# Attention and two mixtures on one core: q, k and v in longer runs, the weights' clamp as two operations, the norm's refinement in two instructions

## The chip, the cores and the metric

The kernel runs on one core of one Trainium2 chip. The metric is the device time of one execution in microseconds (us). Each kernel was run three times; the median is quoted. Beside the timed runs one execution was profiled; its trace is what is read here.

## What is computed

Three steps follow one another. Shapes: q, k and v are 4 x 8 x 576 x 64 (batch, head, token, dimension), the token matrix is 2304 x 512.

```python
def _attn_ref(q, k, v, g_norm):
    kv = np.einsum('bhsd,bhse->bhde', k, v)
    out = np.einsum('bhsd,bhde->bhse', q, kv)
    rms = np.sqrt(np.mean(out * out, axis=-1, keepdims=True) + 1e-06)
    return (out / rms * g_norm).astype(np.float32)

def _moe_ref(x, w1, w2, w3, w_out):          # 512 -> 768 -> 512
    h = np.maximum(np.maximum(x @ w1, x @ w2), x @ w3)
    return (h @ w_out).astype(np.float32)

def _moe2_ref(x, domain_probs, w1, w2):      # 4 experts, 512 -> 1024 -> 512
    p = domain_probs / (domain_probs.sum(-1, keepdims=True) + 1e-09)
    out = np.zeros((N, D), dtype=np.float32)
    for e in range(E):
        h = np.maximum(x @ w1[e], 0.0)
        out += p[:, e:e + 1] * (h @ w2[e])
    return out.astype(np.float32)
```

The weights of the middle step arrive as 64-bit floats, all other inputs as 32-bit floats.

## The kernel before

The kernel has one fixed order of work. A list of short step names (`steps`, near the end of the program) sets the order in which all engines get their instructions up to about 150 us; behind it come the long loops of matrix products, which the change doesn't touch.

**Loads.** After each step `pump()` issues whatever loads the list `order` has next, as long as a buffer is free: `kbc` is the load of k and v for batch b and the c-th four heads (`load_kv`), `qn` the load of the n-th group of queries (`load_q`), `w` the next weight of the middle step. All go through SP's queue, apart from v's first half, which goes through ACT's. There are three pairs of k/v buffers and six q buffers. The program's waits also hold every load until the one issued eight loads before it has landed.

**How q, k and v lie in the chip's memory.** 576 tokens are 4.5 times 128. For k and v, partition p holds the four tokens 4p to 4p+3 of each head, one run of 1 KB, and the last 64 tokens go to the first 64 partitions in a second, small load of 256 B runs. For q a group is 256 tokens of one batch, partition p holding two tokens, a run of 512 B; the last 64 tokens of all four batches form group 2, the tail, loaded by four DMAs to 32 partitions each.

**Attention steps.** `Kbc` (`att_kv`) forms k-transposed times v for a pair of heads: ten matmuls, five chunks of tokens times two heads. Behind the last pair of a batch its result is copied into `kvb`. `Tn` (`att_T`) transposes the queries of group n on PE and copies them out; for the tail POOL first reorders them into `qr`. `On` (`att_O`) multiplies them with `kvb`, squares on ACT and sums on DVE, and forms `a`, the mean square plus epsilon. `Nn` (`att_N`) takes the inverse root: ACT's square root `s0`, DVE's reciprocal, one refinement `s0 + a/s0` (two instructions), another reciprocal, and the scaling. `Xn` (`att_X`) transposes the result back for the next step, and `Sj` splits it into a high and a low part.

**Weights.** A weight goes through `c` (`conv0`: ACT takes the absolute value of the upper words, POOL clamps them), `d` (`conv1`: DVE builds the 32-bit float with three instructions) and `s` (`conv2`: split into two parts on ACT, POOL or DVE). There are 24 weights, c0 to c23; c0 runs at 11 us, c1 and c2 near 46 us, the others between 64 and 152 us, beside the products of the middle step (steps A, H, P).

The output rows: `tiles` holds, for each 128-row tile, the rows of `out` it is written to; the token order within a batch follows that of q. The probabilities are loaded in the same order by `load_probs`.

Of the kernel before, what the change touches and what calls it, by code (L numbers as in the profile page):

```python
# [21 lines left out]
def tile_attn_moe_moe2(  # L22
# [109 lines left out]
    def load_q(pool, gi):
        b, s0, _ = groups[gi]
        t = pool.tile([P, H, 2, D], F32, tag="q", name=f"q{gi}", bufs=6)
        if s0 is None:
            n = P // B
            for bb in range(B):
                nc.sync.dma_start(
                    out=t[bb * n : (bb + 1) * n], in_=q[bb, :, SB:S, :].rearrange("h (p r) d -> p h r d", r=2)
                )  # L140
        else:
            nc.sync.dma_start(
                out=t, in_=q[b, :, s0 : s0 + 256, :].rearrange("h (p r) d -> p h r d", r=2)
            )
        q_sb[gi] = t

    HALF = P // 2
    KS = P * KC  # L150

    def load_first(pool):

        ends = []
        for src, nm, eng in ((k, "k", nc.sync), (v, "v", nc.scalar)):
            t = pool.tile([P, 4, KC + 1, D], F32, tag="kv", name=f"{nm}0_0", bufs=6)
            rows = src[0, 0:4]
            parts = [
                (t[:, 2 * i : 2 * i + 2, 0:KC, :], rows[2 * i : 2 * i + 2, 0:KS, :].rearrange("h (p c) d -> p h c d", c=KC))
                for i in range(2)  # L160
            ]
            eng.dma_start(out=parts[0][0], in_=parts[0][1])
            eng.dma_start(out=t[0:HALF, :, KC, :], in_=rows[:, KS:S, :].rearrange("h p d -> p h d"))
            ends.append(parts[1])
            kv_sb[nm, 0, 0] = t
# [3 lines left out]
    def load_kv(pool, b, c):
        if (b, c) == (0, 0):  # L170
            return load_first(pool)
        for src, nm in ((k, "k"), (v, "v")):
            t = pool.tile([P, 4, KC + 1, D], F32, tag="kv", name=f"{nm}{b}_{c}", bufs=6)
            rows = src[b, 4 * c : 4 * c + 4]
# [97 lines left out]
    def att_kv(kvb, b, c, eng=""):  # L272
        if c == 0:
            kv_ps[b] = banks[7]
        ps = kv_ps[b]
        kt, vt = kv_sb["k", b, c // 2], kv_sb["v", b, c // 2]
        for i in range(KC + 1):
            for h in range(2):
                o = ps[h * D : (h + 1) * D, c * D : (c + 1) * D]
                n = P if i < KC else HALF  # L280
                hh = c % 2 * 2 + h
                nc.tensor.matmul(o, kt[0:n, hh, i, :], vt[0:n, hh, i, :], start=(i == 0), stop=(i == KC))
        if c == NPAIR - 1:
            dst = kvb[b % 2][:, 0 : H * P].rearrange("p (c h n) -> p c h n", h=2, n=P)
            for h in range(2):
                src = ps[h * D : (h + 1) * D, 0 : NPAIR * D].rearrange("p (c e) -> p c e", e=D)
                e = eng[2 * h :] or "aa"
                copy(e[0], dst[0:D, :, h, 0:D], src)
                copy(e[1], dst[D:P, :, h, D:P], src)

    qT = {}
    TAIL = 2
    xtok = {}

    def att_T(pool, gi, eng="aa"):


        pair = groups[gi][1] is None
        t = pool.tile([P, 4, P, 2] if pair else [P, 2, 4, P], F32, tag="qp" if pair else "qT", name=f"qT{gi}", bufs=1 if pair else 2)
        qs = q_sb.pop(gi)  # L300
        if pair:
            qr = pool.tile([P, 2, H, D], F32, tag="qr", name="qr", bufs=1)
            nc.gpsimd.tensor_copy(out=qr, in_=qs.rearrange("p h r d -> p r h d"))
        for i in range(2):
            ps = bank("a").rearrange("p (c n) -> p c n", n=P)
            for c in range(4):
                src = qr[:, i, 2 * c : 2 * c + 2, :] if pair else qs[:, 4 * i + c, :, :]
                nc.tensor.transpose(ps[:, c, :], src, ident)
            copy(eng[i], t[:, :, :, i] if pair else t[:, i], ps)
        qT[gi] = t  # L310

    def att_O(pool, kvb, gi):
        b, s0, _ = groups[gi]
        qt = qT[TAIL] if s0 is None else qT.pop(gi)
        ps = [bank("acc") for i in range(1 if s0 is None else 2)]
        xt = pool.tile([P, 2, H, D], F32, tag="xt", name=f"xt{gi}", bufs=3)
        if s0 is None:
            nbank = 1
            for c in range(NPAIR):
# [19 lines left out]
        def small(nm):  # L339
            return smp.tile([P, nbank, 8], F32, tag=nm, name=f"{nm}{gi}")  # L340

        ss, a = small("ss"), small("a")
        for i in range(nbank):
            sq = xt[:, i]
            nc.scalar.activation(out=sq, in_=o[i], func=AF.Square)
            nc.vector.reduce_sum(out=ss[:, i, :], in_=sq, axis=AX.X)
        nc.vector.tensor_scalar(out=a, in0=ss, scalar1=1.0 / D, scalar2=EPS, op0=ALU.mult, op1=ALU.add)
        xtok[gi] = (xt, ss, a, o, dst, small)

    def att_N(gi):  # L350
        xt, ss, a, o, dst, small = xtok[gi]
# [42 lines left out]
    nm = [0]  # L394
# [80 lines left out]
    first = [1]  # L475
# [424 lines left out]

    def norm_probs():
# [374 lines left out]
```

## Time and profile before

| what | value |
|---|---|
| median of 3 runs | 1102.78 us (1101.92 to 1104.07) |
| the profiled execution | 1102.58 us |
| its span in the trace | 1100.8 us |
| PE busy | 1070.6 us (97%) |
| DVE busy | 768.7 us (70%) |
| ACT busy | 593.9 us (54%) |
| POOL busy | 238.8 us (22%) |
| DMA queue of SP | 89,248 packets, 169.34 MB |

PE is the matrix engine, PEld its weight loads, DVE the vector engine, ACT the scalar engine, POOL GpSimd; SPq is SP's queue, which issues DMAs. The shares are means over the whole span. The first 62 us are attention; until 150 us the middle step runs beside the conversion of its weights; everything behind that is matrix products. Rows of the trace name lines of the program, as L282, and in brackets the time for which the engine stood idle before a row and what ended the wait.

### The profile page before, as it was taken

To read this page: it belongs to the slowest core of one execution; us is meant where nothing else is said; L and a number is where in the kernel's file an instruction comes from. 1 tells how busy PE (TensorE), PEld (TensorE's weight loads), DVE (VectorE), ACT (ScalarE), POOL (GpSimd) and SP (SyncE) were. 2 spreads that over 40 slices of the span, in tenths; PEclk is the share of its full clock that TensorE was granted. 3 is DMA by queue.
4 is the path that set the end of the run, shared out by engine and by line. 5 is a ranking of instruction groups with operands and counts; after the bars stand their busy time and mean duration, and the time that the engine had idled before them with its cause. 6 is when DMAs were issued, how large, how long until landed. Compare 5 with 4: busy or idle time off the path is not lost.

```text
span 1100.8 us, 19219 instructions
## 1 busy us (share of the span) xinstructions
PE 1070.6 (97%) x7318; PEld 1051.7 (96%) x7318; DVE 768.7 (70%) x1434; ACT 593.9 (54%) x1257; POOL 238.8 (22%) x269
## 2 busy tenths in 40 slices
PE   7889999999999989999999999999999999999997
PEld 6779999999999879999999999999999999999997
DVE  3889985667656879776676666667667666666556
ACT  3544224335343666665665566666566566556652
POOL 1336633330101101111202212212212220221121
PEclk8999999999999999999999999999999999999999
DMA  9945555431610877388569579759949957956875
GB/s 259 295 148 162 181 182 178 132 119 53 210 58 20 328 270 266 142 311 240 90 221 272 119 169 285 182 100 290 250 77 277 277 86 227 271 116 166 235 222 115
DMA packets 109820, 209.17 MB, mean 190 GB/s; under 512 B 13856, under 2 KB 67104, under 8 KB 109728
## 3 DMA queue, kind: packets, MB, share of 16 engines
q1 hardware_dynamic: 89248, 169.34, 46.4%
q0 software_dynamic: 19472, 37.76, 19.2%
q8 instruction: 57, 0.93, 0.3%
q10 hardware_dynamic: 1008, 0.85, 0.3%
q14 instruction: 35, 0.29, 0.1%
HBM read 137.93 MB, written 69.99 MB: 189 GB/s over the span
## 4 chain that ended last, share of the span: by engine, by line
PE 63%; DVE 0%; issue 0%; DVEq 0%
PE bank L878 32%; PE bank L617 30%; DVE wr L579 0%; DVE xr L500 0%; DVE fa L861 0%; DVE hr L653 0%; DVE hr L651 0%; DVEq L1271 0%
## 5 line engine op out<-in xcount | busy, mean ns | idle before, releaser
L878 PE MATMUL bank<-wr 128*128 128x256 f32 x1701 | 263.5, 283 | 0.4 <-DVE wr L579 0.4
L878 PEld LDWEIGHTS bank<-wr 128*128 128x128 f32 x1701 | 239.9, 190 | 0.6 <-DVE wr L579 0.6
L617 PE MATMUL bank<-rb,wl 128*128 128x384 f32 x1032 | 211.6, 340 | 4.2 <-DVE rb L500 2.3
L671 ACT ACTIVATE fa<-bank 128x384 f32<-128x384 f32 x192 | 94.7, 493 | 171.4 <-PE bank L617 169.5
L617 PEld LDWEIGHTS bank<-rb,wl 128*128 128x128 f32 x1032 | 176.0, 189 | 7.4 <-DVE rb L500 3.5
L617 PE MATMUL bank<-xr,wl 128*128 128x384 f32 x864 | 175.8, 337 | 1.7 <-DVE xr L500 1.1
L617 PEld LDWEIGHTS bank<-xr,wl 128*128 128x128 f32 x864 | 144.9, 188 | 3.6 <-DVE xr L500 2.5
L653 DVE TENSOR_TENSOR wr<-fa,wr 128x384 fp32r<-128x384 f32 x131 | 72.3, 552 | 50.8 <-ACT wr L646 50.7
L878 PE MATMUL bank<-wr,hr 128*128 128x256 f32 x558 | 91.0, 281 | 0.0
L836 POOL DMA_DIRECT2D out_dram<-w2s x48 | 48.1, 1027 | 193.0 <-DVE ob L861 145.0
L836 POOL DMA_DIRECT2D out_dram<-ob x48 | 47.7, 1033 | 166.8 <-DVE w2s L861 90.6
L878 PEld LDWEIGHTS bank<-wr,hr 128*128 128x128 f32 x558 | 80.5, 188 | 0.0
L646 ACT ACTIVATE wr<-fa 128x384 fp32r<-128x384 f32 x152 | 78.2, 529 | 2.0 <-DVE fa L661 0.5
L878 PE MATMUL bank<-wr,xr 128*128 128x256 f32 x405 | 67.9, 281 | 0.0
L760 DVE TENSOR_TENSOR fa<-bank,fa 128x384 f32<-128x384 f32 x54 | 29.9, 554 | 51.8 <-ACT fa L757 36.5
L836 POOL DMA_DIRECT2D out_dram<-fa x37 | 34.2, 1054 | 123.9 <-DVE fa L861 68.9
L694 DVE TENSOR_TENSOR fa<-bank,fa 128x384 f32<-128x384 f32 x48 | 26.7, 557 | 49.2 <-PE bank L617 49.2
L683 DVE TENSOR_TENSOR fa<-bank,fa 128x384 f32<-128x384 f32 x48 | 26.7, 557 | 48.0 <-ACT fa L671 47.2
L859 ACT ACTIVATE ob<-bank,p_all 128x256 f32<-128x256 f32 x102 | 48.3, 474 | 21.7 <-PE bank L878 20.0
L859 ACT ACTIVATE w2s<-bank,p_all 128x256 f32<-128x256 f32 x104 | 49.3, 474 | 18.8 <-PE bank L878 18.7
L617 PE MATMUL bank<-op,wl 128*128 128x384 f32 x288 | 58.7, 339 | 0.6 <-ACT fa L671 0.6
L878 PEld LDWEIGHTS bank<-wr,xr 128*128 128x128 f32 x405 | 59.0, 188 | 0.0
(207 smaller groups left out, 2041.9 us busy)
## 6 DMA issues: line engine op xcount, KB each, us to landing
rb<-op_d SPq DMA_DIRECT2D x42, 768.0 KB, 5.1
xr<-op_d SPq DMA_DIRECT2D x42, 768.0 KB, 7.0
out_dram<-w2s POOLq DMA_DIRECT2D x47, 256.0 KB, 5.9
out_dram<-ob POOLq DMA_DIRECT2D x46, 256.0 KB, 5.2
op<-op_d SPq DMA_DIRECT2D x14, 768.0 KB, 7.9
stage_a<-in_moe_w_dram SPq DMA_DIRECT2D x18, 512.0 KB, 4.0
w1s<-in_moe_w_dram SPq DMA_DIRECT2D x30, 256.0 KB, 3.6
out_dram<-fa POOLq DMA_DIRECT2D x30, 256.0 KB, 5.9
```

The costliest lines, as they stand in the source:

```text
L617: nc.tensor.matmul(out, w[wi][:, c * P : (c + 1) * P], y[yi][:, c, :], start=(i == 0 and k in begin), stop=(i == 5), skip_group_check=k no ...
L646: nc.scalar.activation(out=ops[key][0], in_=src, func=AF.Relu if relu else AF.Copy)
L653: nc.vector.tensor_tensor(out=lo, in0=src, in1=f32(hi), op=ALU.subtract)
L671: nc.scalar.activation(out=out, in_=in_, func=func)
L683: nc.vector.tensor_tensor(out=t22, in0=x, in1=t22, op=ALU.add)
L694: nc.vector.tensor_tensor(out=t12, in0=x, in1=t12, op=ALU.add)
L760: nc.vector.tensor_tensor(out=mx[done] if i == 0 else t, in0=x, in1=t, op=ALU.add)
L836: nc.gpsimd.dma_start(out=rows, in_=src, accum_op=ALU.add)
L859: nc.scalar.activation(out=o, in_=piece(ps, i), func=AF.Copy, scale=pe)
L878: nc.tensor.matmul(piece(ps, i), h[hi][:, i * P : (i + 1) * P], w[wi], start=fresh, stop=last, skip_group_check=True,)
```

## The change

Four things are edited, all in the part up to 150 us.

- **k and v**: partition p of 96 holds the six tokens 6p to 6p+5 of each head, one run of 1.5 KB. The small second load is gone; `att_kv` has twelve matmuls (six chunks times two heads), each over 96 partitions.
- **q**: one tile holds a whole batch's first 512 tokens, partition p four of them, a run of 1 KB, loaded in two DMAs of four heads each; it serves two groups. There are three such tiles. The tail is loaded in eight DMAs with 256 B runs, already in the order that the transposes want, so POOL's copy `qr` goes. The list `order` is shortened to match; `out`'s rows and the probabilities follow the new order of tokens (rows 8 KB apart instead of 4 KB, still 2 KB each).
- **The clamp** on POOL: `min` becomes `min` and then `max` with 0.0, which changes no value, since these are absolute values.
- **The norm**: `a` is no longer formed; the refinement is two instructions of the form (x op constant) op y, the first one from the sum `ss` itself.

The core of the diff:

```diff
-    KC = S // P
+    KC = 6
+    KP = S // KC
...
     def load_q(pool, b):
+        if b == B:
+            t = pool.tile([P, 2, H, D], F32, tag="qe", name="q_ends", bufs=1)
             n = P // B
             for bb in range(B):
+                for r in range(2):
+                    nc.sync.dma_start(
+                        out=t[bb * n : (bb + 1) * n, r],
+                        in_=q[bb, :, SB:S, :].rearrange("h (p r) d -> r p h d", r=2)[r],
+                    )
+            q_sb[TAIL] = t
+            return
+        t = pool.tile([P, H, 4, D], F32, tag="q", name=f"q{b}", bufs=3)
+        for i in range(2):
+            hs = slice(i * H // 2, (i + 1) * H // 2)
+            nc.sync.dma_start(out=t[:, hs], in_=q[b, hs, 0:SB, :].rearrange("h (p r) d -> p h r d", r=4))
...
+    def load_kv(pool, b, c):
...
+            t = pool.tile([P, 4, KC, D], F32, tag="kv", name=f"{nm}{b}_{c}", bufs=6)
+            rows = src[b, 4 * c : 4 * c + 4].rearrange("h (p c) d -> p h c d", c=KC)
...
+                nc.sync.dma_start(out=t[0:KP], in_=rows)
-            nc.sync.dma_start(out=t[:, :, 0:KC, :], in_=rows[:, 0:KS, :].rearrange("h (p c) d -> p h c d", c=KC))
-            nc.sync.dma_start(out=t[0:HALF, :, KC, :], in_=rows[:, KS:S, :].rearrange("h p d -> p h d"))
...
-        nc.gpsimd.tensor_scalar(out=t, in0=t, scalar1=EXP_TOP, scalar2=None, op0=ALU.min)
+        nc.gpsimd.tensor_scalar(out=t, in0=t, scalar1=EXP_TOP, scalar2=0.0, op0=ALU.min, op1=ALU.max)
...
-                nc.tensor.matmul(o, kt[0:n, hh, i, :], vt[0:n, hh, i, :], start=(i == 0), stop=(i == KC))
+                nc.tensor.matmul(o, kt[0:KP, hh, i, :], vt[0:KP, hh, i, :], start=(i == 0), stop=(i == KC - 1))
...
-            nc.gpsimd.tensor_copy(out=qr, in_=qs.rearrange("p h r d -> p r h d"))
...
-        nc.vector.tensor_scalar(out=a, in0=ss, scalar1=1.0 / D, scalar2=EPS, op0=ALU.mult, op1=ALU.add)
...
-        nc.vector.tensor_tensor(out=rr, in0=a, in1=rr, op=ALU.mult)
-        nc.vector.tensor_tensor(out=rr, in0=rr, in1=s0, op=ALU.add)
+        nc.vector.scalar_tensor_tensor(out=rr, in0=ss, scalar=EPS * D, in1=rr, op0=ALU.add, op1=ALU.mult)
+        nc.vector.scalar_tensor_tensor(out=rr, in0=rr, scalar=1.0 / D, in1=s0, op0=ALU.mult, op1=ALU.add)
...
-            "w k00 k01 q1 q0 k10 q3 q2 k11 q4 q5 k20 w q6 k21 w k30 k31 q8 w q9"
+            "w k00 k01 q0 k10 q4 k11 q1 k20 w q2 k21 w k30 k31 w q3"
...
-        free = {"q": 6, "k": 3}
+        free = {"q": 4, "k": 3}
```

The edit of the load list moves loads on SP's queue. Before, from the first queries to the loads that step K12 needs (k_0 and k_1 are names of buffers, a number behind a DMA's shape says how often it is issued):

```order
L142 DMA q_193<-in_q_dram 128x8x128
L142 DMA q_195<-in_q_dram 128x8x128
L175 DMA k_0_197<-in_k_dram 128x4x256
L176 DMA k_0_197<-in_k_dram 64x4x64
L175 DMA v_0_200<-in_v_dram 128x4x256
L176 DMA v_0_200<-in_v_dram 64x4x64
L142 DMA q_203<-in_q_dram 128x8x128
L138 DMA q_205<-in_q_dram 32x8x128 x4
L175 DMA k_1_233<-in_k_dram 128x4x256
L176 DMA k_1_233<-in_k_dram 64x4x64
L175 DMA v_1_236<-in_v_dram 128x4x256
L176 DMA v_1_236<-in_v_dram 64x4x64
```

The same stretch of SP's queue with the change, up to the second batch's queries:

```order
L151 DMA q_189<-in_q_dram 128x4x256 x2
L165 DMA k_0_192<-in_k_dram 96x4x384
L165 DMA v_0_194<-in_v_dram 96x4x384
L142 DMA q_ends<-in_q_dram 32x8x64 x8
L165 DMA k_1_232<-in_k_dram 96x4x384
L165 DMA v_1_234<-in_v_dram 96x4x384
L151 DMA q_236<-in_q_dram 128x4x256 x2
```

Step T3's queries were q_203, 512 KB ahead of the tail and of K12's k and v; now they are half of q_236, 1 MB behind both.

On PE the steps X1, T2, T3, K12 and K13, before:

```order
L375 MATMUL bank_71<-ident,xt_294 128x128 x4
L375 MATMUL bank_72<-ident,xt_294 128x128 x4
L308 MATMUL bank_70<-ident,qr 128x128 x4
L308 MATMUL bank_71<-ident,qr 128x128 x4
L308 MATMUL bank_72<-ident,q_203 128x128 x4
L308 MATMUL bank_70<-ident,q_203 128x128 x4
L282 MATMUL bank_73<-v_1_236,k_1_233 64x64 x20
```

and with the change:

```order
L360 MATMUL bank_71<-ident,xt_293 128x128 x4
L360 MATMUL bank_72<-ident,xt_293 128x128 x4
L294 MATMUL bank_70<-ident,q_ends 128x128 x4
L294 MATMUL bank_71<-ident,q_ends 128x128 x4
L294 MATMUL bank_72<-ident,q_236 128x128 x4
L294 MATMUL bank_70<-ident,q_236 128x128 x4
L272 MATMUL bank_73<-v_1_234,k_1_232 64x64 x24
```

PE's order of steps is the same; K12 and K13 grow from 20 matmuls to 24 and stay behind T3, whose queries now come last.

On DVE the sums of groups 2 and 4 and the start of N2, before (`a` is L347):

```order
L346 TENSOR_REDUCE ss_493<-xt_484 128x8
L347 TENSOR_SCALAR a_494<-ss_493 128x8
L346 TENSOR_REDUCE ss_528<-xt_519 128x8 x2
L347 TENSOR_SCALAR a_529<-ss_528 128x16
L356 RECIPROCAL rr_539<-s_538 128x8
L357 TENSOR_TENSOR rr_539<-a_494,rr_539 128x8
L358 TENSOR_TENSOR rr_539<-rr_539,s_538 128x8
```

and with the change:

```order
L332 TENSOR_REDUCE ss_488<-xt_479 128x8
L332 TENSOR_REDUCE ss_523<-xt_514 128x8 x2
L341 RECIPROCAL rr_532<-s_531 128x8
L342 SCALAR_TENSOR_TENSOR rr_532<-ss_488,rr_532 128x8
L343 SCALAR_TENSOR_TENSOR rr_532<-rr_532,s_531 128x8
```

One small instruction of each of the ten groups leaves DVE's queue; nothing else on it moves.

## Rows read from the trace of the kernel before

**Rows 1.** Busy time by stretch: length, then PE, PEld, DVE, ACT, POOL, clock, DMA, GB/s

```profile
10.00:20.00 10.00, 7.40 (x62) 6.56 (x63) 2.50 (x4) 2.55 (x6) 1.73 (x2) 0.66 1.13 288
38.00:62.00 24.00, 20.78 (x264) 18.18 (x264) 22.66 (x50) 12.39 (x27) 7.63 (x7) 1.00 1.13 307
62.00:150.00 88.00, 83.59 (x498) 80.74 (x499) 82.79 (x131) 34.25 (x62) 51.72 (x41) 0.98 0.51 159
```

**Rows 2.** PE's waits from 0 to 62 us: total, times, longest

```profile
PE bank L282 <- DMA v<-in_v_dram: 5.9, 5, 2.9
PE bank L308 <- POOL qr L303: 1.8, 1, 1.8
```

**Rows 3.** DMA view of single microseconds, from 5, 8, 13 and 22 us

```profile
DMA packets 622, 0.25 MB, mean 252 GB/s; under 512 B 491, under 2 KB 622, under 8 KB 622
DMA packets 343, 0.35 MB, mean 350 GB/s; under 512 B 1, under 2 KB 343, under 8 KB 343
DMA packets 607, 0.30 MB, mean 304 GB/s; under 512 B 14, under 2 KB 607, under 8 KB 607
DMA packets 403, 0.20 MB, mean 196 GB/s; under 512 B 20, under 2 KB 403, under 8 KB 403
```

**Rows 4.** DMA view: us to landing of the issues at 8.58 and 24.43

```profile
v<-in_v_dram SPq DMA_DIRECT2D x1, 64.0 KB, 4.3
v<-in_v_dram SPq DMA_DIRECT2D x1, 64.0 KB, 6.5
```

**Rows 5.** Timeline of SP's queue: start, us, line

```profile
8.58 0.61 SPq L176 DMA_DIRECT2D v<-in_v_dram  x1
...
24.43 0.61 SPq L176 DMA_DIRECT2D v<-in_v_dram  x1
```

**Rows 6.** Timeline of PE: steps K02 and K03, T3, K12 and K13, X6

```profile
12.58 2.98 PE L282 MATMUL bank<-v,k 128*64 128x64 f32 x40 [2.94 <-DMA v<-in_v_dram]
...
29.07 1.12 PE L308 MATMUL bank<-ident,q 128*128 128x128 f32 x8
30.58 1.82 PE L282 MATMUL bank<-v,k 128*64 128x64 f32 x40 [0.39 <-DMA v<-in_v_dram]
...
63.21 1.10 PE L375 MATMUL bank<-ident,xt 128*128 128x128 f32 x6 [2.09 <-ACT qT L69]
```

**Rows 7.** Timeline of POOL and DVE around the norm's `a`

```profile
37.06 1.26 POOL L210 TENSOR_TENSOR wl<-cv_a,wl 128x512 fp32r<-128x512 f32 x1
37.43 0.92 DVE L347 TENSOR_SCALAR a<-ss 128x16 f32<-128x16 f32 x1
38.27 1.74 DVE L389 TENSOR_TENSOR xr<-fa,xr 128x1536 fp32r<-128x1536 f32 x1
...
54.94 0.83 DVE L347 TENSOR_SCALAR a<-ss 128x16 f32<-128x16 f32 x1
56.98 0.17 DVE L347 TENSOR_SCALAR a<-ss 128x16 f32<-128x16 f32 x1
61.70 0.43 DVE L71 COPY kvb<-bank 64x256 f32<-64x256 f32 x1
```

**Rows 8.** Groups by line and shape, 0 to 160 us: busy, mean ns, idle before

```profile
L225 POOL TENSOR_SCALAR cv_a<-cv_a 128x512 f32<-128x512 f32 x18 | 28.7, 1592 | 32.4 <-ACT cv_a L224 31.7 <-DVE fa L405 0.7
L71 POOL CAST wr<-cv_o 128x512 fp32r<-128x512 f32 x3 | 1.8, 607 | 0.0
L210 POOL TENSOR_TENSOR wl<-cv_a,wl 128x512 fp32r<-128x512 f32 x6 | 8.0, 1338 | 0.8 <-ACT wl L69 0.4
L233 DVE SCALAR_TENSOR_TENSOR cv_a<-stage_a,cv_a 128x512 int32<-128x512 int32 x18 | 14.7, 817 | 0.6
L236 DVE SCALAR_TENSOR_TENSOR cv_o<-stage_o,cv_o 128x512 int32<-128x512 int32 x6 | 4.1, 691 | 0.2
```

**Rows 9.** PE's waits from 62 to 150 us: total, times, longest

```profile
PE bank L375 <- ACT qT L69: 2.1, 1, 2.1
PE bank L260 <- DVE fa L405: 1.5, 2, 1.3
PE bank L375 <- DVE xt L366: 0.9, 1, 0.9
PE bank L424 <- DVE xt L366: 0.8, 1, 0.8
```

More of the change, by code (lines that the diff above doesn't have):

```diff
@@ L59, in tile_attn_moe_moe2 @@
     NPAIR = H // 2
-    KC = S // P
+    KC = 6
+    KP = S // KC
     EPS = 1e-6
+    HALF = P // 2
     WARM = 16
@@ L118, in tile_attn_moe_moe2 @@
     groups = []
-    SB = S // 256 * 256
+    SB = S // 512 * 512
+    TAIL = 2
+    by_r = [out[b * S : b * S + SB, :].rearrange("(p r) d -> r p d", r=4) for b in range(B)]
     for b0 in range(0, B, 2):
@@ L125, in tile_attn_moe_moe2, with load_q @@
             else:
-                rows = out[b * S + s0 : b * S + s0 + 256, :].rearrange("(p r) d -> r p d", r=2)
-                tiles += [[rows[0]], [rows[1]]]
+                r0 = s0 // P
+                tiles += [[by_r[b][r0]], [by_r[b][r0 + 1]]]
     q_sb = {}
     kv_sb = {}
[L132 to L135, printed above, removed]
+    def load_q(pool, b):
+        if b == B:
+            t = pool.tile([P, 2, H, D], F32, tag="qe", name="q_ends", bufs=1)
@@ L136, in load_q @@
             n = P // B
             for bb in range(B):
[L138 to L152, printed above, removed]
-        ends = []
[L155 to L165, printed above, removed]
+                for r in range(2):
[3 more added lines that the diff above has]
+                    )
@@ new lines, in load_q @@
+            q_sb[TAIL] = t
[4 more added lines that the diff above has]
+            nc.sync.dma_start(out=t[:, hs], in_=q[b, hs, 0:SB, :].rearrange("h (p r) d -> p h r d", r=4))
+        for n, gi in enumerate(gi for gi, g in enumerate(groups) if g[0] == b and g[1] is not None):
+            q_sb[gi] = t[:, :, 2 * n : 2 * n + 2, :]
+    def load_kv(pool, b, c):
+        first = (b, c) == (0, 0)
+        ends = []
+        for src, nm in ((k, "k"), (v, "v")):
+            t = pool.tile([P, 4, KC, D], F32, tag="kv", name=f"{nm}{b}_{c}", bufs=6)
+            rows = src[b, 4 * c : 4 * c + 4].rearrange("h (p c) d -> p h c d", c=KC)
+            if first:
+                (nc.sync if nm == "k" else nc.scalar).dma_start(out=t[0:KP, 0:2], in_=rows[:, 0:2])
+                ends.append((t[0:KP, 2:4], rows[:, 2:4]))
+            else:
+                nc.sync.dma_start(out=t[0:KP], in_=rows)
+            kv_sb[nm, b, c] = t
@@ L166, in load_first @@
         for o, i in ends:
             nc.sync.dma_start(out=o, in_=i)
[L169 to L174, printed above, removed]
-            nc.sync.dma_start(out=t[:, :, 0:KC, :], in_=rows[:, 0:KS, :].rearrange("h (p c) d -> p h c d", c=KC))
-            nc.sync.dma_start(out=t[0:HALF, :, KC, :], in_=rows[:, KS:S, :].rearrange("h p d -> p h d"))
-            kv_sb[nm, b, c] = t
@@ L276, in att_kv @@
         kt, vt = kv_sb["k", b, c // 2], kv_sb["v", b, c // 2]
-        for i in range(KC + 1):
+        for i in range(KC):
             for h in range(2):
                 o = ps[h * D : (h + 1) * D, c * D : (c + 1) * D]
-                n = P if i < KC else HALF
                 hh = c % 2 * 2 + h
-                nc.tensor.matmul(o, kt[0:n, hh, i, :], vt[0:n, hh, i, :], start=(i == 0), stop=(i == KC))
+                nc.tensor.matmul(o, kt[0:KP, hh, i, :], vt[0:KP, hh, i, :], start=(i == 0), stop=(i == KC - 1))
         if c == NPAIR - 1:
@@ L291, in tile_attn_moe_moe2 @@
     qT = {}
-    TAIL = 2
     xtok = {}
@@ L300, in att_T @@
         qs = q_sb.pop(gi)
-        if pair:
-            qr = pool.tile([P, 2, H, D], F32, tag="qr", name="qr", bufs=1)
-            nc.gpsimd.tensor_copy(out=qr, in_=qs.rearrange("p h r d -> p r h d"))
         for i in range(2):
@@ L306, in att_T @@
             for c in range(4):
-                src = qr[:, i, 2 * c : 2 * c + 2, :] if pair else qs[:, 4 * i + c, :, :]
+                src = qs[:, i, 2 * c : 2 * c + 2, :] if pair else qs[:, 4 * i + c, :, :]
                 nc.tensor.transpose(ps[:, c, :], src, ident)
@@ L340, in small @@
             return smp.tile([P, nbank, 8], F32, tag=nm, name=f"{nm}{gi}")
-        ss, a = small("ss"), small("a")
+        ss = small("ss")
         for i in range(nbank):
@@ L346, in att_O @@
             nc.vector.reduce_sum(out=ss[:, i, :], in_=sq, axis=AX.X)
-        nc.vector.tensor_scalar(out=a, in0=ss, scalar1=1.0 / D, scalar2=EPS, op0=ALU.mult, op1=ALU.add)
-        xtok[gi] = (xt, ss, a, o, dst, small)
+        xtok[gi] = (xt, ss, o, dst, small)
     def att_N(gi):
-        xt, ss, a, o, dst, small = xtok[gi]
+        xt, ss, o, dst, small = xtok[gi]
         nbank = len(o)
@@ L895, in load_probs @@
             else:
-                r0 = b * S + s0
+                r0 = s0 // P
                 nc.sync.dma_start(
-                    out=p_all[:, t : t + 2, :], in_=probs[r0 : r0 + 256, :].rearrange("(p r) e -> p r e", r=2)
+                    out=p_all[:, t : t + 2, :],
+                    in_=probs[b * S : b * S + SB, :].rearrange("(p r) e -> p r e", r=4)[:, r0 : r0 + 2, :],
                 )
@@ L926, in tile_attn_moe_moe2 @@
         order = (
-            "w k00 k01 q1 q0 k10 q3 q2 k11 q4 q5 k20 w q6 k21 w k30 k31 q8 w q9"
+            "w k00 k01 q0 k10 q4 k11 q1 k20 w q2 k21 w k30 k31 w q3"
         ).split()
-        free = {"q": 6, "k": 3}
+        free = {"q": 4, "k": 3}
+        got = set()
         def pump():
@@ L997, in tile_attn_moe_moe2 @@
                 att_T(xq, *at, *en)
-                free["q"] += 1
+                mate = {0: 1, 1: 0, 3: 4, 4: 3, 5: 6, 6: 5, 8: 9, 9: 8}.get(at[0])
+                got.add(at[0])
+                free["q"] += mate in got
             elif kind == "K":
```

## The prediction

> **What bounds the kernel now.** I read the stretches first. Beyond 150 us the change touches no instruction of PE, which is 97% busy over the span, so the question is how much earlier or later that part starts. Between 62 and 150 us PE is busy for 83.6 of 88 us and DVE for 82.8 [rows 1]: both are nearly full, and a shift at 62 us is passed on to the end, with no slack to swallow it. From 38 to 62 us DVE is busy for 22.7 of 24 us [rows 1] and runs without a wait from 38.27 to the copy at 61.70 [rows 7]; PE then waits 2.09 us for what that copy frees [rows 6]. So DVE is the bound there, and PE (20.8 of 24) isn't. Before 38 us neither is full: PE waits 5.9 us for v, most of it once, at 12.58, and 1.8 us for POOL's copy of the tail [rows 2, 6]. There the chain runs through PE's order: T2, T3, K12 and K13, then X0 and the split whose last instruction is DVE's at 38.27. What this chain gains or loses stays to the end.
>
> **Prices of a load.** In a microsecond in which the 16 DMA engines are busy, 16,000 ns divided by the packets is what one packet takes of an engine: 1 KB 16,000/343 = 46.6 ns, 512 B 16,000/607 = 26.4 ns, and 256 B (16,000 - 131 x 46.6)/491 = 20.2 ns [rows 3]. By the step from 512 B to 1 KB, 1.5 KB would take 66.8 ns, an estimate. One load of k or v was 512 packets of 1 KB and 256 of 256 B, 29.0 us of engine time or 1.81 us on sixteen engines. It becomes 384 packets of 1.5 KB: 1.60 us, if 96 partitions cost nothing. At 22 us, where the tail's DMAs run, each over 32 partitions, the same 512 B packets moved at 196 GB/s instead of 304 [rows 3]: a quarter of the partitions, 0.645 of the rate. Two thirds of the way back to 128 partitions is 0.88, which makes 1.82 us; in proportion to the partitions it would be 2.13 us. I take 1.82, nearest to the only row on fewer partitions: k and v gain nothing. Ends 1.60 and 2.13.
>
> [...]
>
> **T3's queries.** Before, the last data on this chain was K12's v: ahead of it a weight (512 packets, 1.49 us), eight loads of k and v (14.5), three groups of q (1024 x 26.4/16 = 1.69 each, 5.1) and the tail (524 KB at 196 GB/s, 2.7), 23.8 us together. It was issued at 24.43 and landed 6.5 later, at 30.9 [rows 4, 5], 7.1 behind the sum. Now T3, ahead of K12 on PE, needs the whole second batch: a weight 1.49, eight loads 14.6, two batches of q (1024 x 46.6/16 = 2.98 each, 6.0) and the tail 2.7, 24.8 us. With the same lag it lands at 31.9. But at 12.9 (8.58 + 4.3) [rows 4, 5] the lag was only 12.9 - 1.49 - 4 x 1.81 = 4.2; the other 2.9 came between, while half of the eight loads in flight were small ones. Now they are large, the tail's eight aside; I give half of it back: 30.4. The second half of T3 ran at about 29.6 [rows 6], so T3 is 0.8 late. K12 and K13 take 1.82 us for 40 rows, so 48 take 2.18, another 0.4 [rows 6]. **X0 and DVE's run: 1.2 us later.** Ends: lag 4.2 at 1.60 us a load gives 27.2, so 2.0 us earlier; full lag at 2.13 gives 34.4, so 5.2 later. T2 no longer waits for POOL (1.8 us), but T3 waits right behind it, so this gives nothing in the sum. PE's eight K steps between 38 and 58 us cost 8 x 0.18 = 1.5 us more and lie beside DVE's run; if that cover goes, PE's waits for v and q there (over 2 us) do, too.
>
> **The norm.** `a` goes in ten groups. Five lie in or at DVE's run: those of 0.17 us (three, like the one at 56.98), the one of 0.83 at 54.94, and the one of 0.92 at 37.43 [rows 7]. The last gives nothing: POOL's instruction from 37.06 to 38.32 would hold the next one, too. With a gap of 0.04 each: **1.5 us earlier** (ends 0.7, if what follows waits for POOL at 55 us as well, and 2.4). What replaces the two refinements is the same size on the same data; the three-operand form takes 691 ns for 512 columns where nothing disturbs it [rows 8], so I cost it at nothing (±0.04 us x 20). Of the other groups, three run between 62 and 150 us: **0.5 us**, since PE waits for DVE only now and then there.
>
> **The clamp.** POOL's 512 columns take 1592 ns, more than its instruction with two inputs (1338), while a cast of the same data takes 607 [rows 8]. So moving the data isn't what it pays for; the one-operation form is dear by itself. No row shows the form with two. Ends: 0.61 us, the cast, and 2.98, twice a clamp undisturbed at 1.49. I take 0.61 as the likelier, by the nearest row that reads and writes the same data, but as a case with its own chance. Of POOL's 51.7 us between 62 and 150 us, 21 clamps are 33; 21 x 0.98 = 21 would go. DVE's instructions stretch beside POOL's: L233 takes 817 ns on average against 691 for the same form undisturbed [rows 8], 2.3 us over 18, and two more of a conversion are exposed, some 7 us in all. Two fifths of POOL's work gone would give 2.8 us back, and PE can use at most 3.2, its waits for DVE there [rows 9], the 2.1 belonging to the run above. **2.2 us earlier**; c0 to c2 lie beside other work. Nothing (0) if the form costs the same.
>
> **Sum**, from the profiled execution, 1102.58 us (span 1100.8 and 1.8 around it; the median is 1102.78): + 1.2 - 1.5 - 0.5 - 2.2 = 1099.6. The output rows' new order costs nothing: as many runs of 2 KB, and no engine waits for them.
>
> **The rivals.**
> - *The loads do get faster*: 1.60 us a load, lag 4.2: X0 2.0 earlier instead of 1.2 later. 1102.6 - 2.0 - 1.5 - 0.5 - 2.2 = 1096.4. For it speaks the 350 GB/s of 1 KB packets, against it the row at 22 us.
> - *The clamp costs what it did*: 1099.6 + 2.2 = 1101.8.
> - *T3 comes late (slower)*: 2.13 us a load and the full lag put its queries at 34.4, X0 5.2 later. [...] Another 1.2: 1102.6 + 6.4 - 4.2 = 1104.8. It is slower than before as soon as X0 comes over 4.2 us later, or over 2.0 with the old clamp (then 1107.0).
> - *The clamp gets dearer (slower)*: 2.98 us, 29 us more on POOL, 81 of 88 busy; DVE's 7 us of stretching grow by over half and POOL's queue stands between ACT and DVE: some 6 us. 1102.6 + 1.2 - 2.0 + 6 = 1107.8. It decides from about 2 us a clamp.
>
> **How the numbers follow.** Forecast 0.34; faster loads 0.17; same clamp 0.26; late T3 0.15; dearer clamp 0.08. I predict 1099.6. The forecast's own range is 1097.5 to 1101.5. Without the dearer clamp and the ends of late T3 and faster loads, eight in ten lie between 1095.8 and 1105.5. A difference of 0.2% (2.2 us) is about what a measurement can tell. Faster: 0.25 of the forecast, all of faster loads, 0.04 of the same clamp, 0.46. Slower: 0.09 of late T3, 0.08, and 0.03 of the same clamp, 0.20. Same: 0.34.
>
> **What the profile will show.** Loads: packets of 1.5 KB near 310 GB/s or 370, and the landing of the second batch's queries (30.4). Chain: T3's row with its wait, X0 near 33.5 instead of 32.3, DVE's split at 39.5. Norm: DVE's run 1.5 us shorter. Clamp: the mean of POOL's rows, 0.61, 1.5 or 3, and PE's waits for DVE behind 62 us. Wrong it would be if DVE's run isn't the bound, so that the K steps on PE show, or if the clock falls where it didn't before.

## The result: the changed kernel is slower

The changed kernel takes 1109.8 us (median of 5 runs, 1107.9 to 1114.2), the kernel before 1103.45 beside it: ratio 1.0069, 95% interval [1.0043, 1.0095]. By the ratio it is 7.6 us slower, by the two medians 6.4; 1099.6 was predicted, and it lies above the range. Its five executions fall into two clusters, three at 1108 to 1110 and two at 1114, which is why the interval is wide. The profiled execution took 1109.8 us, span 1108.0, 7.2 over that of before.

Where the time went, first by stretches of the changed kernel: length, then PE, PEld, DVE, ACT, POOL, clock, DMA, GB/s.

```profile
10.00:20.00 10.00, 5.43 (x76) 4.75 (x76) 2.15 (x4) 1.27 (x4) 0.50 (x1) 0.52 1.11 246
20.00:38.00 18.00, 12.12 (x113) 10.83 (x114) 8.99 (x20) 6.01 (x12) 0.00 (x0) 0.78 1.06 223
38.00:62.00 24.00, 22.09 (x270) 20.35 (x271) 16.70 (x33) 14.10 (x29) 6.39 (x7) 0.86 1.11 257
62.00:80.00 18.00, 14.10 (x160) 12.82 (x158) 11.80 (x25) 8.55 (x17) 4.08 (x6) 0.81 0.64 190
62.00:150.00 88.00, 82.27 (x570) 79.46 (x569) 78.52 (x130) 34.42 (x64) 37.14 (x41) 0.96 0.54 160
207.00:1000.00 793.00, 785.20 (x5248) 776.79 (x5247) 551.35 (x1044) 460.13 (x987) 139.43 (x171) 1.00 0.64 188
```

Against [rows 1], the DMA engines are about as busy as before from 38 to 62 us (1.11, before 1.13) and move 257 GB/s where it was 307. DVE, which was full from 38 to 62 us (22.66), now has 7 us idle there, and the granted clock is 0.86 instead of 1.00. From 80 to 150 us PE is busy for 68.2 of 70 us (before 66.8), and from 207 us (200 before) for the same 99% as before:

```profile
200.00:993.00 793.00, 785.46 (x5243) 777.56 (x5242) 550.16 (x1043) 459.24 (x986) 136.68 (x170) 1.00 0.65 188
```

So the loss arises ahead of 80 us, where the loads run. PE's waits of the changed kernel, 0 to 62 us, and behind them the rows of T3, K12 with K13, and X0 on PE's timeline:

```profile
PE bank L294 <- DMA q<-in_q_dram: 6.2, 3, 3.4
PE bank L272 <- DMA v<-in_v_dram: 5.4, 2, 3.5
```

```profile
34.61 1.09 PE L294 MATMUL bank<-ident,q 128*128 128x128 f32 x4 [3.43 <-DMA q<-in_q_dram]
37.95 1.08 PE L294 MATMUL bank<-ident,q 128*128 128x128 f32 x4 [2.25 <-DMA q<-in_q_dram]
38.97 2.83 PE L272 MATMUL bank<-v,k 96*64 96x64 f32 x48
41.73 1.54 PE L360 MATMUL bank<-ident,xt 128*128 128x128 f32 x6
```

T3 is L294, and its second half starts at 37.95; before, T3's row was 29.07, K12 and K13 followed at 30.58 [rows 6], and X0 stood at 32.33:

```profile
32.33 1.09 PE L375 MATMUL bank<-ident,xt 128*128 128x128 f32 x8
```

X0 is 9.4 us later. Single microseconds of the changed kernel's DMA view: one with k and v nearly alone (18 us), one with them quite alone (20 us), and one with the queries' 1 KB packets on 128 partitions (33 us):

```profile
DMA packets 143, 0.21 MB, mean 210 GB/s; under 512 B 3, under 2 KB 143, under 8 KB 143
DMA packets 160, 0.24 MB, mean 243 GB/s; under 512 B 2, under 2 KB 160, under 8 KB 160
DMA packets 358, 0.35 MB, mean 350 GB/s; under 512 B 16, under 2 KB 358, under 8 KB 358
```

A load of k or v (590 KB) thus took some 2.4 to 2.8 us of all sixteen engines, 2.6 at 230 GB/s, not 1.82. One more row stood out, on SP's queue, where the eight DMAs of the tail were spread over 12 us and k11 came behind them:

```profile
13.29 12.17 SPq L142 DMA_DIRECT2D q_ends<-in_q_dram  x8
25.61 0.34 SPq L165 DMA_DIRECT2D k<-in_k_dram  x1
```

What held SP there were the program's own waits for earlier loads to land (3.1 us for k, 2.4 for v, 1.2 for q), by its limit of eight. At 25.15 us, when the last DMA of the tail went out, small DMAs alone were under way. From 22 to 25 us they moved 156 GB/s, and from 25 to 26 us, before k11's data came, the DMA engines were busy for 0.42 only (last two columns):

```profile
22.00:25.00 3.00, 3.00 (x20) 3.00 (x19) 0.69 (x1) 1.11 (x2) 0.00 (x0) 0.64 1.32 156
25.00:26.00 1.00, 1.00 (x27) 0.83 (x27) 0.88 (x2) 0.24 (x2) 0.00 (x0) 1.00 0.42 55
```

### The profile page after: what moved, and what is told of

Read it like the earlier page. It is cut to its first block, busy times and chain, and to the rows that moved or that the text cites. A ratio compares the mean times of both kernels' runs of the same rounds, so it can differ in the third digit from the quotient of the medians.

```text
span 1108.0 us, 19319 instructions
## 1 busy us (share of the span) xinstructions
PE 1073.6 (97%) x7382; PEld 1056.4 (95%) x7382; DVE 765.0 (69%) x1424; ACT 594.2 (54%) x1257; POOL 221.8 (20%) x268
## 4 chain that ended last, share of the span: by engine, by line
PE 82%; DVE 8%; DMA 5%; ACT 2%; issue 1%; SPq 0%; POOL 0%; DVEq 0%; ACTq 0%
PE bank L602 42%; PE bank L863 32%; PE bank L769 4%; DMA q<-in_q_dram 2%; PE bank L409 2%; PE bank L251 1%; DMA q_ends<-in_q_dram 1%; DMA k<-in_k_dram 1%; DVE rb L485 1%; DVE cv_a L224 1%; DMA w_da<-cv_a 1%; DVE cv_o L224 1%; DMA stage_o<-in_moe_w_out_dram 0%; DVE cv_a L227 0%; DVE fa L579 0%
```

## The experiments

Three theories. **Partitions**: a transfer to 96 partitions is slow, whatever its packets. **Packets**: packets of 1.5 KB are slow. **Issue**: SP, held at the tail's eight DMAs, issues k11 and the second batch of queries too late. Each kernel ran 4 to 12 times here, beside 15 to 24 executions of the kernel before on the same chip (5 beside 5 for the changed kernel); since the median of that one varied from 1103.4 to 1104.4, the last column is the ratio times 1102.6, the scale on which expectations are written.

| kernel | us, median | ratio, 95% interval | on the scale of 1102.6 |
|---|---|---|---|
| changed kernel | 1109.8 | 1.0069 [1.0043, 1.0095] | 1110.2 |
| e1: clamp and norm | 1098.98 | 0.9955 [0.9942, 0.9968] | 1097.6 |
| e2: loads (k, v and q) | 1113.14 | 1.0077 [1.0065, 1.0090] | 1111.1 |
| e3: k and v on 96 | 1116.45 | 1.0100 [1.0083, 1.0118] | 1113.6 |
| e4: queries | 1106.5 | 1.0018 [1.0009, 1.0026] | 1104.6 |
| e5: e2, 128 partitions | 1106.96 | 1.0022 [1.0011, 1.0033] | 1105.0 |
| e6: e2, packets of 1 KB | 1118.07 | 1.0131 [1.0114, 1.0148] | 1117.0 |
| e7: e4, old tail | 1107.36 | 1.0031 [1.0020, 1.0042] | 1106.0 |
| e8: e4, other order | 1107.15 | 1.0028 [1.0017, 1.0038] | 1105.7 |
| e9: clamp | 1102.39 | 0.9983 [0.9972, 0.9993] | 1100.7 |
| e10: e1, two heads on 128 | 1096.79 | 0.9934 [0.9921, 0.9947] | 1095.3 |
| e11: changed, two heads on 128 | 1100.94 | 0.9978 [0.9968, 0.9989] | 1100.2 |
| e12: e10, T2 behind X0 | 1095.3 | 0.9925 [0.9912, 0.9939] | 1094.3 |

**The parts alone.** e1 takes the diff's lines of the clamp, `att_O` and `att_N` over into the kernel before; e9 the clamp's line alone:

```diff
-        nc.gpsimd.tensor_scalar(out=t, in0=t, scalar1=EXP_TOP, scalar2=None, op0=ALU.min)
+        nc.gpsimd.tensor_scalar(out=t, in0=t, scalar1=EXP_TOP, scalar2=0.0, op0=ALU.min, op1=ALU.max)
```

> The kernel before with the pair of operations in the clamp and the two-instruction refinement, its loads as they were. The prediction's steps for these two parts (1.5 and 0.5 us from the norm, 2.2 us from the clamp) give 1102.6 - 4.2 = 1098.4 us. Rival: POOL and DVE only become idler and PE's waits behind 62 us stay, since something else than DVE ends them; then 1101.5 to 1103.

> The kernel before with the clamp as a pair of operations and nothing else. By the prediction's step for the clamp 2.2 us earlier than before (ratio 0.998), so that of e1's 5 us the norm has 2.8. Rival: the clamp is worth all of it (PE's and DVE's waits for POOL behind 62 us), ratio 0.9955 as e1; or nothing, ratio 1.000, if only DVE's run ahead of 62 us counts.

Together they gain 5.0 us, the clamp 1.9 of it, so 3.1 are the norm's, give or take 1.9 by the two intervals. POOL's groups of the clamp, first of e9, then of the changed kernel (busy, mean ns, idle before):

```profile
L225 POOL TENSOR_SCALAR cv_a<-cv_a 128x512 f32<-128x512 f32 x18 | 15.3, 848 | 40.7 <-ACT cv_a L224 40.7
```

```profile
L216 POOL TENSOR_SCALAR cv_a<-cv_a 128x512 f32<-128x512 f32 x18 | 13.5, 749 | 40.4 <-ACT cv_a L215 40.4
```

1592 ns before [rows 8], 848 and 749 now: on average the pair costs half of the single operation. The means hold longer instructions (three of 1.80 to 2.03 us before, five of 1.04 to 1.15 in the changed kernel); the median of the 18 was 1496 ns before and is 620 in e9 and 616 in the changed kernel, which is the 0.61 us that the prediction took from the cast. The norm shows in DVE's run, from the split's end to the copy of kvb. Rows of e9, with `a` still an instruction, and of e1:

```profile
39.95 1.75 DVE L389 TENSOR_TENSOR xr<-fa,xr 128x1536 fp32r<-128x1536 f32 x1
63.40 0.42 DVE L71 COPY kvb<-bank 64x256 f32<-64x256 f32 x1
```

```profile
39.01 2.63 DVE L388 TENSOR_TENSOR xr<-fa,xr 128x1536 fp32r<-128x1536 f32 x1
62.08 0.43 DVE L71 COPY kvb<-bank 64x256 f32<-64x256 f32 x1
```

From 41.70 to 63.40 is 21.7 us, from 41.64 to 62.08 is 20.4: 1.3 us shorter. The split began 0.94 earlier and ended at the same time: it took 2.63 us in e1 where it took 1.75 in e9.

**The loads alone.** e2 is the changed kernel with the old clamp and norm; e3 the kernel before with the new `load_kv` and K steps; e4 the changed queries with the old `load_kv` and K steps, clamp and norm. e2 and e3, and e5 and e6 below, also keep two buffers instead of four for `s0` and `rr`; DVE's wait for the square root in them is 0.5 us where it was 0.7 before, so this cost nothing there.

> The changed kernel with the old clamp (one operation) and the old norm (a in an instruction of its own): the loads, the order of the loads and the matmuls with 96 rows alone. If the clamp and the norm are worth 4.2 us and add up with the loads, it takes the changed kernel's 1109.8 + 4.2 = 1114 us, so the loads cost some 11.5 us where the prediction put +1.2. Rival: clamp and norm are worth nothing behind late loads; then 1109.5 to 1110.5.

> The kernel before with k and v alone loaded in runs of 1.5 KB on 96 partitions and multiplied in six steps of 96 rows; queries, their order, clamp and norm as before. Theory of the rate (a load on 96 partitions takes 2.5 to 2.6 us of the DMA engines instead of 1.8): eight loads ahead of K12 take 5.6 to 6.4 us more, X0 stands 5 to 7 us later, and the time is 1107.5 to 1109.5. Theory of the issue (SP, held up by the eight small DMAs of the tail, issues k11 and q1 too late): the tail is as before, so nothing is lost: 1101.5 to 1104.

> The changed kernel's queries alone (runs of 1 KB for a whole batch, the tail in eight DMAs of 256 B runs, their new order), with k, v, clamp and norm as before. Theory of the rate: only the tail and the order differ, X0 within 3 us of before, 1101.5 to 1105. Theory of the issue: SP is held at the tail as in the changed kernel and PE's wait at T3 stays, X0 6 to 9 us later: 1108 to 1111.

e2, at 1111.1, lies between its two cases (1114 if clamp and norm add up with the loads, 1109.5 to 1110.5 if they are worth nothing behind them), nearer to the second. The queries alone cost 2.0 us, inside the range of the theory of the rate; k and v alone cost 11.0, more than either theory had. The issue theory gave e3 nothing and e4 most of the loss, and both came out the other way. In e3 T3 runs without a wait, but K12 waits for v, and PE's waits for v go on behind X0 (L361, 38.33):

```profile
36.00 2.40 PE L268 MATMUL bank<-v,k 96*64 96x64 f32 x48 [2.08 <-DMA v<-in_v_dram]
38.33 1.87 PE L361 MATMUL bank<-ident,xt 128*128 128x128 f32 x8
40.03 2.00 PE L318 MATMUL bank<-kvb,qT 128*128 128x128 f32 x16
41.96 1.09 PE L310 MATMUL bank<-kvb,qT 128*64 128x128 f32 x16
45.68 0.92 PE L268 MATMUL bank<-v,k 96*64 96x64 f32 x24 [2.63 <-DMA v<-in_v_dram]
```

PE's waits of e3, 0 to 80 us:

```profile
PE bank L268 <- DMA v<-in_v_dram: 18.7, 7, 4.3
```

X0 shows a part of these 18.7 us only: once the loads are behind, v is late again and again (seven waits), not once. X0 itself, at 38.33, is 6.0 us late, as that theory had it; that it stopped there is where my 1107.5 to 1109.5 fell short. With the queries in long runs, too (e2), 2.5 us come back.

**Partitions or packets.** e5 and e6 move the bytes of e2, once over 128 partitions in 1.5 KB packets, once over 96 in 1 KB packets. In both the rows lie where the matmuls don't look for them, so they are there for their times only; e5, which fills three of the four heads' places, lets the fourth head's matmuls read the first place:

```diff
-            rows = src[b, 4 * c : 4 * c + 4].rearrange("h (p c) d -> p h c d", c=KC)
+            rows = src[b, 4 * c : 4 * c + 4].rearrange("h (p c) d -> (h p) c d", c=KC).rearrange("(j p) c d -> p j c d", j=3)
...
-                nc.sync.dma_start(out=t[0:KP], in_=rows)
+                nc.sync.dma_start(out=t[:, 0:3], in_=rows)
...
-                hh = c % 2 * 2 + h
+                hh = (c % 2 * 2 + h) % 3
```

```diff
-            rows = src[b, 4 * c : 4 * c + 4].rearrange("h (p c) d -> p h c d", c=KC)
+            rows = src[b, 4 * c : 4 * c + 4].rearrange("h (p c) d -> (h p) c d", c=4).rearrange("(j p) c d -> p j c d", p=KP)
...
-                nc.sync.dma_start(out=t[0:KP], in_=rows)
+                t6 = t[0:KP].rearrange("p h c d -> p (h c) d").rearrange("p (j c) d -> p j c d", c=4)
+                nc.sync.dma_start(out=t6, in_=rows)
```

> The kernel of e2 (changed loads alone) with every load of k and v spread over 128 partitions: the same bytes in the same 384 packets of 1.5 KB, three to a partition. The rows then lie where the matmuls don't look for them (they still multiply 96 rows in six steps, three of the four heads' places), so k^T v isn't the reference's. Theory of the partitions (96 of 128 make a load slow): loads move at 340 to 380 GB/s as the 1 KB packets of q do, PE's waits for v and q ahead of X0 shrink by 5 us or more, 1104 to 1107. Theory of the packets (1.5 KB packets are slow wherever they go): rates stay at 220 to 250 GB/s, 1112 to 1114. Theory of the issue (SP held by the tail's DMAs): k11 and q1 are issued as late as before, 1109 to 1113.

> The kernel of e2 with every load of k and v on 96 partitions still, but in 576 packets of 1 KB, six to a partition (rows again where the matmuls don't look for them). Theory of the partitions: as slow as e2 or slower, 220 to 250 GB/s, 1112 to 1115. Theory of the packets (1.5 KB is the dear size): 340 to 350 GB/s as with q's 1 KB packets, 1104 to 1107.

A microsecond with k and v alone, in e5 (10 us) and in e6 (12 us):

```profile
DMA packets 265, 0.40 MB, mean 399 GB/s; under 512 B 5, under 2 KB 265, under 8 KB 265
```

```profile
DMA packets 188, 0.19 MB, mean 193 GB/s; under 512 B 0, under 2 KB 188, under 8 KB 188
```

In these microseconds the same 1.5 KB packets move at 399 GB/s over 128 partitions and at 210 to 243 over 96; packets of 1 KB at 350 over 128 (queries, above) and at 193 over 96. The partitions decide; the size is worth 14% on 128 of them (399 for 350). The time follows: e5 is 6.1 us faster than e2, e6 5.9 slower. e5 and e4 issue the tail in the same eight DMAs and cost 2.4 and 2.0 us, so the issue theory can explain a small part of the loss at most. X0 shows the same shares. Its rows in e2, e4, e5 and, from further below, e11 (the changed kernel with k and v on 128 partitions):

```profile
41.27 1.88 PE L361 MATMUL bank<-ident,xt 128*128 128x128 f32 x8
36.63 1.97 PE L375 MATMUL bank<-ident,xt 128*128 128x128 f32 x8
34.43 1.97 PE L361 MATMUL bank<-ident,xt 128*128 128x128 f32 x8
35.99 1.16 PE L359 MATMUL bank<-ident,xt 128*128 128x128 f32 x8
```

With 128 partitions X0 comes 6.8 us earlier (e5 against e2) and 5.7 (e11 against the changed kernel); without the 96 it is still 2 to 4 us later than before, through the queries, their order and the tail. Each is one profiled execution, and X0 stands at 34.0 in e9 and e1, whose loads are those of before (32.33), so a difference of under 2 us between two traces proves little.

**Tail and order.** e7 is e4 with the tail's four DMAs (its expectation says two) and POOL's copy of before; e8 is e4 with

```diff
-            "w k00 k01 q0 k10 q4 k11 q1 k20 w q2 k21 w k30 k31 w q3"
+            "w k00 k01 q0 k10 q1 k11 q4 k20 w q2 k21 w k30 k31 w q3"
```

> The kernel of e4 (queries in runs of 1 KB, all else as before) with the tail loaded as before: two DMAs of 512 B runs and POOL's copy. Theory of the issue (the eight DMAs of the tail hold SP and use the engines at 150 GB/s): T3's wait of 3.62 us falls below 2 and X0 comes 1.5 us earlier than 36.63, 1104 to 1105.5. Rival (T3 waits because the whole second batch now comes behind K11's loads and the tail, whatever the tail's form): the wait stays, and T2 waits for POOL's copy besides, 1106 to 1108.

> The kernel of e4 with one edit in the order of the loads: the second batch of queries ahead of k11, and the tail behind k11. Theory of the order: T3 no longer waits for its queries, T2 waits for the tail instead by 1 to 3 us, X0 at 34 to 35.5 in place of 36.63, 1103.5 to 1105.5. Theory of the issue: the tail's eight DMAs now stand ahead of T2 and K20 and the wait only changes its name, 1106 to 1108.

Neither gains: their intervals overlap with e4's, and both medians are above it. In e8 the wait only changed its name, from T3 for q (3.62 us) to T2 for the tail:

```profile
30.93 1.67 PE L308 MATMUL bank<-ident,q_ends 128*128 128x128 f32 x8 [4.06 <-DMA q_ends<-in_q_dram]
```

In e7 k11 is issued at 17.74 us instead of 22.72 in e4, yet T3's wait fell only from 3.62 to 2.95 and X0 came 1.15 us earlier, with nothing of it left at the end: the issue theory is tested here and fails. Why the long queries cost 2.0 us was not settled beyond this: that T3 waits for a whole batch where it waited for a group.

**Long runs on all partitions.** A head's 576 rows as 64 runs of 9 rows (2304 B), two heads one above the other: e10 puts this into e1, e11 into the changed kernel.

```diff
-            t = pool.tile([P, 4, KC, D], F32, tag="kv", name=f"{nm}{b}_{c}", bufs=6)
-            rows = src[b, 4 * c : 4 * c + 4].rearrange("h (p c) d -> p h c d", c=KC)
...
+            t = pool.tile([P, 2, KC, D], F32, tag="kv", name=f"{nm}{b}_{c}", bufs=6)
+            for m in range(2):
+                i = src[b, 4 * c + 2 * m : 4 * c + 2 * m + 2].rearrange("h (p c) d -> (h p) c d", c=KC)
...
-                nc.tensor.matmul(o, kt[0:KP, hh, i, :], vt[0:KP, hh, i, :], start=(i == 0), stop=(i == KC - 1))
+                hs = slice(h * HALF, (h + 1) * HALF)
+                nc.tensor.matmul(o, kt[hs, c % 2, i, :], vt[hs, c % 2, i, :], start=(i == 0), stop=(i == KC - 1))
```

> e1 (clamp and norm changed, queries as before) with k and v in long runs that fill all 128 partitions: a head's 576 rows lie in runs of 9 (2304 B) on 64 partitions, and two heads lie one above the other, so a load is 256 packets. K's steps are nine of 64 rows for each head. If 96 partitions were what made the long runs slow, these load at 370 to 400 GB/s, 1.5 us a load instead of 1.8, and PE's waits for v ahead of X0 (4.5 us in e1) shrink by 2 us or more: 1096 to 1098 us. Rival 1: nine steps of 64 rows take PE longer than five (72 rows of the timeline for two K steps instead of 40) and eat it: 1099 to 1101. Rival 2: packets beyond 2 KB are slow whatever their partitions: 1102 or more.

> The changed kernel whole (its queries, tail, order of loads, clamp, norm) with one edit: k and v lie two heads one above the other on 128 partitions, as in e10, instead of on 96. If the 96 partitions are the cause, this alone turns the change round: e10's 1096.8 plus the 2 us that e4 showed for the queries, 1098 to 1100 against 1109.8. Rival (the queries' order and the tail are half of the loss): 1102 to 1106.

This edit alone turns the changed kernel round: e11 is 10.0 us faster than it, and 2.4 faster than before; at 1100.2 it ends just above the 1098 to 1100 expected. The edit also changes the size of the packets and makes two DMAs of each load, so that the partitions alone are to blame rests on e5. e10, at 1095.3 a little below its 1096 to 1098, gains 2.3 us on e1, though the ends of their intervals overlap, and is 4.9 faster than e11. What separates these two are the long queries with their order and tail, which cost 2.0 in e4; why they cost more here was not looked for. Of e10: PE's longest wait for v in the first microseconds (steps K02 and K03), the stretch from 10 us, and a microsecond of its loads (39 us):

```profile
10.91 2.31 PE L267 MATMUL bank<-v,k 64*64 64x64 f32 x72 [0.90 <-DMA v<-in_v_dram]
```

```profile
10.00:20.00 10.00, 7.39 (x143) 6.87 (x144) 4.48 (x8) 3.61 (x8) 0.82 (x2) 1.00 1.06 309
```

```profile
DMA packets 191, 0.39 MB, mean 392 GB/s; under 512 B 21, under 2 KB 21, under 8 KB 191
```

392 GB/s, so packets of 2304 B aren't slow (rival 2). Two K steps take 2.31 us where it was 1.82 [rows 6] (rival 1 is right there), eight times over, and it costs less than the loads give. PE waits 0.90 us there where it waited 2.94 before [rows 6], and the granted clock stays at 1.00 through a stretch where its mean was 0.66 before [rows 1] and 0.52 in the changed kernel. There it had fallen to 0.50 already about the end of an earlier wait for v, 1.96 us up to 10.71, ahead of the wait of 3.5 us. The changed kernel's row behind that wait, and its stretches from 10 and 11 us (the clock is the third number from the end):

```profile
10.71 1.55 PE L272 MATMUL bank<-v,k 96*64 96x64 f32 x24 [1.96 <-DMA v<-in_v_dram]
10.00:11.00 1.00, 0.29 (x6) 0.32 (x8) 0.43 (x2) 0.00 (x0) 0.50 (x1) 0.75 1.10 226
11.00:12.00 1.00, 1.00 (x24) 1.00 (x21) 0.97 (x2) 0.00 (x0) 0.00 (x0) 0.50 1.11 246
```

**T2 behind X0.** In e10 PE waits 2.61 us for POOL's copy of the tail at T2, ahead of X0. e12:

```diff
-X1 N0 T2 T3.va K12 K13.vvaa X0.va O3 S0.pv
+X1 N0 T3.va K12 K13.vvaa X0.va T2 O3 S0.pv
```

> e10 with one edit in PE's order: the transposes of the tail (T2), which wait 2.6 us for POOL's copy there, go behind X0. If T3's queries and K12's k and v have landed by then (in e10 T3 runs at 28.4 and K12 at 30.0 with no wait of their own), X0 comes 2 to 4 us earlier and the time falls to 1093 to 1095.5. Rival (the wait only changes its name: T3 or K12 waits for a DMA instead, or DVE's run is then held by the tail's split): 1096 to 1097.5.

T2 now runs after X0; K12 waits 1.64 us for v instead, and X0 is at 29.21, 3.0 us earlier than in e10 (32.22):

```profile
26.96 2.31 PE L267 MATMUL bank<-v,k 64*64 64x64 f32 x72 [1.64 <-DMA v<-in_v_dram]
29.21 1.09 PE L359 MATMUL bank<-ident,xt 128*128 128x128 f32 x8
30.14 0.60 PE L293 MATMUL bank<-ident,qr 128*128 128x128 f32 x4
```

On the median it is 1.0 us ahead of e10 by the ratios, and the intervals overlap. It is the fastest kernel here, 8.3 us faster than before. e1, e9, e10 and e11 beat both kernels, too, e10 and e12 by the most.

## Why the prediction was wrong

The step that failed is the first one, **"Prices of a load"**, and through it "X0 and DVE's run: 1.2 us later". It took 1.82 us for a load on 96 partitions, with an end at 2.13, "in proportion to the partitions". Measured is 2.6, beyond both ends: 0.58 of the rate on 128 partitions (230 of 399 GB/s) for 0.75 of the partitions. My interpolation from 32 partitions (0.645) to 128 put 96 at 0.88; the measured share lies below even that of the row on 32 partitions. Why the rate falls so far, no run shows.

**T3's queries.** The list of transfers was right, its prices weren't. With 2.56 us for each of the eight loads (590 KB at 230 GB/s), the prediction's own sum is 1.5 + 20.5 + 6.0 + 2.7 = 30.7, and with its lag of 5.6 (chosen) or 7.1 (full) the queries land at 36.3 or 37.8; T3's second half started at 37.95. So the lag hadn't shrunk much: giving half of it back was a second, smaller miss of at most 1.5 us. That the full lag meets 37.95 so closely is luck, for the tail was mis-sized, too: put at 2.7 us by the 196 GB/s of before, it moved its 524 KB in smaller packets at 156 GB/s, 3.4 us. e4, which loads k and v as before, shows these smaller misses by themselves: T3's second half starts at 32.70 instead of 30.4, and X0 is 4.3 us later than before instead of 1.2. The rival "T3 comes late (slower)" named the mechanism, the late queries, and was priced at 5.2 us of X0 instead of 9.4; at 1104.8 it ended 5 us too low. Its other 1.2 us are those of K02 and K03 before, 2.98 us instead of 1.82 [rows 6], and came about as put: K12 and K13 took 2.83 us for 48 rows at a granted clock of 0.50 (38 to 42 us), two K steps 1.62 at 1.00 (from 62.41). The rival's chance of 0.15 was too small, since its condition was the one price for which I had no row between 32 and 128 partitions.

**Behind X0.** The prediction's own condition for failing, "if DVE's run isn't the bound", came true: DVE has 16.7 of 24 us from 38 to 62. PE waits for v and q until 70 us, and the step X6 comes at 75.31 instead of 63.21 [rows 6], 12.1 us late. A late wait and X6 in the changed kernel, and X6 in e2:

```profile
66.34 1.62 PE L272 MATMUL bank<-v,k 96*64 96x64 f32 x48 [2.32 <-DMA v<-in_v_dram]
75.31 1.06 PE L360 MATMUL bank<-ident,xt 128*128 128x128 f32 x8
```

```profile
73.52 1.03 PE L361 MATMUL bank<-ident,xt 128*128 128x128 f32 x8
```

So the norm's gain in DVE's run should buy little; that it did is not shown. e1's 5.0 us shrink to 0.9 between e2 and the changed kernel by the ratios, but their intervals allow up to about 4, and the two profiled executions differ by 4.2. Behind X6 the clamp and the rest of the norm seem to count, by one trace of each kernel: from there to the end the changed kernel wins 4.9 us back (12.1 to 7.2), while e2, with the old forms, is 10.3 late at X6 and 11.4 at the end.

**The clamp**: forecast 2.2 us earlier at 0.61 us an instruction; measured 1.9 us alone, at a mean of 0.75 to 0.85 and a median of 0.62. The step held, and of its two ends the nearest row was the right one. **The norm**: 1.5 us in DVE's run, measured 1.3 between two traces; that the 0.92 us in front of the split give nothing held as well. Behind the run 0.5 was put, and 3.1 - 1.3 = 1.8 came, which the uncertainty of the 3.1 (1.9) leaves open; where it lies wasn't looked for. **K steps**: 48 rows of 96 were costed at 2.18 us by the row of before, and take 1.62 at a granted clock of 1.00, less than 40 rows of before (1.82); this erred against the change by 0.56 us for each pair of steps. A row of the changed kernel's PE timeline:

```profile
62.41 1.62 PE L272 MATMUL bank<-v,k 96*64 96x64 f32 x48
```

**The output's order** cost nothing that shows: behind 207 us (200 before) PE is busy alike in the two kernels (785.2 and 785.5 of 793 us).

## What to carry to other kernels

Before a transfer is given longer runs, count the partitions that it still fills: here 128 partitions in packets of 1 KB moved 350 GB/s and 96 in packets of 1.5 KB 210 to 243, k and v on 96 alone (e3) cost 11.0 us, and in a kernel with the right result long runs of k and v paid only when two heads were put one above the other to fill all 128 (e10, 2.3 us ahead of e1; e11, 2.4 ahead of before). Where no row of the trace shows the new partition count, the price of the load is the term that needs the widest ends, since the loads behind it come late, too, not the first only (in e3 PE waits for v seven times, 18.7 us in all). What is to be gained on an engine (DVE's run here) has to be costed again when another step makes that engine wait (DVE was busy for 16.7 of 24 us where it had been for 22.7).

## What the runs showed of the hardware that I had not expected

- Partitions of a DMA: 1.5 KB packets moved at 399 GB/s on 128 partitions (e5, from 10 us) and at 210 to 243 on 96 (changed kernel, from 18 and 20 us), where the mean busy share of the DMA engines was 1.12 and 1.10 (1.06 in e5's). Why was not found.
- GpSimd: a clamp of 128x512 in fp32 takes 1592 ns on average (median 1496) as one operation and 749 to 848 ns (medians 616 and 620) as a pair of operations in one instruction.
- TensorE at a granted clock of 1.00: K's matmuls with 96 rows take 1.62 us for 48, those with 64 rows 2.31 for 72 (34 and 32 ns each), where the mixed steps of 128 and 64 rows took 1.82 for 40 (46 ns).
- Loads of 64 KB under a limit of eight: in the changed kernel the tail's eight DMAs filled the program's limit, their 256 B packets moved at 156 GB/s from 22 to 25 us, and from 25 to 26 us the DMA engines were busy for 0.42 only. e4, which has these DMAs as well, costs 2.0 us in all.
